# A dynamic convolution and a tanh-shrink layer on one core: ScalarE products in the ramp, more helping tokens, two tap sums from superblock 9, and stores ahead of loads

## The chip, the core and the metric

The kernel runs on one core of a Trainium2 chip. The metric is device time in microseconds (us). Seven names are used: TensorE (PE in the profile; its weight loads are PEld), VectorE (DVE), ScalarE (ACT), GpSimd (POOL), SyncE (SP, which here only issues transfers), SBUF (the memory that all engines read) and PSUM (the banks into which TensorE writes).

## The reference

Two stages over 32768 tokens (8 sequences of 4096) of 192 values.

```python
w = softmax(weight_gen, axis=-1)            # 8 heads x 7 taps for each token
x_pad = 6 zero rows ahead of each sequence
conv[s, head] = sum over k of w[s, head, k] * x_pad[s + k, head]   # 24 values a head
h = conv @ w_in                              # 192 x 2048
out = (h - tanh(h)) @ w_out                  # 2048 x 192
```

Inputs and output are float32.

## The kernel before, in words

The tokens are cut into 32 superblocks of 1024 (`TOK`): 128 partitions with 8 tokens (`J`) each. A sequence is four superblocks. The function is one long program, an order written out by hand: each engine takes its instructions in the order in which the code issues them, and waits only where data or a buffer is not ready.

**Making the convolution.** A superblock n needs `x` (8 rows and a halo of 6 in each partition, `load_x`, L144), its seven weights for each token and head (`load_wg`, exp on ScalarE L185, sum L199, reciprocal L208 or L214 and scaling L250 on VectorE or GpSimd), and seven products, one for each tap: x shifted by k times weight k (`tap_product`, L264). GpSimd makes nearly all of them. Taps 0 to 3 go to a tile `pa`, taps 4 to 6 to `pb`, both bf16. `pa` has three buffers, `pb` one. Superblocks 0 and 1 share their products between VectorE (V) and GpSimd (G_) by written lists (L687 and L722).

**Adding the taps.** GpSimd issues transfers that add while they write (`dma_sum`, L256): the first sum adds `pb` to `pa[0:3]`, so that four products are left. For superblocks in `TWO_SUMS` a second sum adds `pa[2:4]` to `pa[0:2]`, so that two are left. The second sum of n is issued after the first products of n + 1 (`second_sum`, L358). TensorE adds what is left while it transposes: `conv_sums` (L419, matmul L436) multiplies every product by the identity into the same PSUM columns, 24 matmuls for each product, and ScalarE evicts to `convT` (L462, in the ramp L454). Superblock 0 and 1 have seven products in this step, 2 and 3 five, 4 to 10 four, 11 and later two.

**The two matmuls.** For each superblock `gemm1` (L474) makes 16 tiles f of 128 of the 2048 columns: six matmuls into a PSUM tile `ph` (three buffers, L496), tanh on ScalarE into `th` (L509), and the difference on VectorE into `gt` (L510). The second matmul, `out_stream` (L550, L564), takes a block of 128 tokens over all 16 `gt`; its two halves of 64 rows run side by side, one block apart, and ScalarE evicts each block (L583). In the loop over n (L803) every step f issues `gemm1(n, f)`, then a number of steps of the second matmul of superblock n - 1 (the `pairs` of a plan), and in between, at the f that the plan names, the transposes of superblock n + 1 (`t2` for its first two chunks of 64 values, `t1` for the third) and the softmax of n + 3 or n + 4.

**Who sets the place of what.** `products(n + 2)` is issued at f = 1 of n; its part `rest` (L359: the products 4 to 6, the first sum, and for superblocks in `LAST_TAP` tap 3 behind that sum) follows later in the step. For superblocks in `LOCKED` the first sum waits for the VectorE instruction of f = 10 (L374). `HELP` (L56, L292) takes tokens from GpSimd: at step f = 3 of n - 2 VectorE makes the product of the last token for taps 0 and 1. `load_x(n + 3)` waits for the first product of n + 2 (`x_after`); its place against the store of superblock n - 1 depends on `STORE_FIRST` (L849, L873): up to n = 8 the store is issued first, later the load. SyncE issues loads and stores in that order.

**Ramp.** Superblock 0's transposes come before any other matmul; ScalarE copies the first 7 of 16 column tiles of `w_in` from the lower to the upper 64 partitions (L712), the rest comes by a transfer (L719). The transposes of superblock 1 lie between the tiles of superblock 0 (`EARLY` and `THIRD`, L742).

**End.** After the last tile the second matmul of the last superblock runs in `gemm2_last` (L598): for each block both halves write one PSUM tile, ScalarE copies the one, VectorE adds the other, and every second block is stored.

Of the kernel before, what the change touches and what calls it, by code (L numbers as in the profile page):

```python
# [8 lines left out]
FP32 = mybir.dt.float32  # L9
# [7 lines left out]
def kernel(  # L17
# [27 lines left out]
    PART = (2, 3)  # L45
    TWO_SUMS = tuple(range(11, 32))
    THREE = ()
    AHEAD = 4
    STORE_FIRST = 8
    EXTRA = (5, 9, 11, 13)  # L50

    WG_AT = 9
    LOCK, LOCKED = 10, tuple(range(14, 32))
    WARM = 0
    SUM_LATE, SUM_BEHIND = (), ()
    HELP = {n: ((n - 2, 3, 2),) for n in range(4, 32)} | {n: ((n - 2, 3, 2), (n - 3, 12, 2)) for n in (9, 10)}  # L56
    CUTS0 = [0, 2, 4]
    LAST_TAP = (4, 5, 6, 7, 8)
    X_LATE = ()
# [3 lines left out]
    RELIEF = ()  # L63
    ACT_OPS = {}
    ACT_AT = {}
    BOTH = False
    RAMP_TAPS = (((True, 6, 7), (False, 2, 6), (True, 0, 2)), ((True, 4, 7), (False, 0, 2), (True, 2, 4)))
    W_CUTS = ((0, 3),)
# [136 lines left out]
    def softmax_recip(n, j0=0, j1=J):  # L205
        if j0 == 0:
            zr_of[n] = wgpool.tile([P, J * H], FP32, name="zr")
        nc.vector.reciprocal(zr_of[n][:, j0 * H : j1 * H], zsum_of[n][:, j0 * H : j1 * H])  # L208

    def softmax_norm(n, bank):  # L210

        wsm = softmax_tile()
        zr_v = bank[:, 512 - J * H : 512]
        nc.vector.reciprocal(zr_v, zsum_of[n][:])  # L214

        def finish():
            scale(nc.vector, wsm[:], e_of[n], zr_v)

        wsm_of[n] = (wsm, None, None, None)
        return finish  # L220
# [60 lines left out]

    def act_product(n, j, k, h):

        x_t, wsm, pa = hold(n)
        nc.scalar.activation(
            out=pa[:, k, j, h * G : (h + 1) * G],
            in_=x_t[:, k + j, h * G : (h + 1) * G],
            func=ACT.Copy,
            scale=wsm[:, j, h, k : k + 1],
        )  # L290

    def help(n, ph, j, kh):  # L292

        x_t, wsm, pa = hold(n)
        w = ph[:, 0, 0 : kh * H].rearrange("p (k h) -> p k h", k=kh)
        nc.vector.tensor_copy(w, wsm[:, j].rearrange("p h k -> p k h")[:, 0:kh])
        tap_product(nc.vector, pa[:, 0:kh], x_t, w, (H, 1), 0, kh, j, j + 1)

    def products(n, taps=None, sums=None, hooks={}):
# [8 lines left out]
        if n == 1:  # L308

            last = [opool.tile([P, 2, J, D], BF16, name="pb1", tag="out_sb") for _ in range(2)]  # L310
            home = [(pa, 0, KA), (last[0], KA, KA + 2), (last[1], KA + 2, K)]
        else:
            pb = pbpool.tile([P, K - KA, J, D], BF16, name="pb")
            home = [(pa, 0, KA), (pb, KA, K)]
# [24 lines left out]

        end = KA - 1 if n in LAST_TAP else KA  # L340
        left = [J - sum(kh > k for _, _, kh in HELP.get(n, ())) for k in range(KA)]
        for j, k in {(j, k) for j, k, _ in ACT_OPS.get(n, ())}:
            left[k] = min(left[k], j)

# [13 lines left out]
        second_sum(n - 1)  # L358
        def rest():  # L359
            if n in PART:  # L360
                dma_sum(pa[:, 0:2], pa[:, 2:4])
            if n - 1 in whole:
                mul(nc.gpsimd, KA, K - 1)
                third_sum(n - 1)
                mul(nc.gpsimd, K - 1, K)
            else:
                mul(nc.gpsimd, KA, K)
            if n in PART:
                prods_of[n] = parts(4, 5, 6, 0, 1)
            else:  # L370
# [4 lines left out]

                if n in LAST_TAP and n in SUM_BEHIND:
                    most(KA - 1, KA)
                    first_sum()
                elif n in SUM_LATE:
                    sum_of[n] = first_sum  # L380
                else:
                    first_sum()
                    if n in LAST_TAP:
                        most(KA - 1, KA)
                if n in TWO_SUMS:
# [8 lines left out]
        return rest  # L394

    def second_sum(n):

        if n in to_sum:
            pa = to_sum.pop(n)
            dma_sum(pa[:, 0:2], pa[:, 2:4])  # L400
            if n in THREE:
                whole[n] = pa

    def third_sum(n):

        if n in whole:
            pa = whole[n]
            dma_sum(pa[:, 0:1], pa[:, 1:2])

    def turn(n):  # L410
# [136 lines left out]
    half = {}  # L547
    out_of = {}

    def out_stream():  # L550
# [46 lines left out]

    def gemm2_last(j, f0=0, f1=NFT):  # L598

        n = NTOT - 1  # L600
        if f0 == 0:
            half[j] = psum_h.tile([P, 2, HT], FP32, name="po2", tag="ph")
        po = half[j]
        col = (j % 2) * HT + (j // 2) * P
        for f in range(f0, f1):
            for r in range(2):
                nc.tensor.matmul(  # L607
# [5 lines left out]
                )  # L613
        if f1 < NFT:
            return
        if j == 0:
            out_of[n] = opool.tile([P, J, D], FP32, name="out_sb")
        out_sb = out_of[n]
        if BOTH:
            nc.vector.tensor_add(out_sb[:, j, :], po[:, 0, 0:D], po[:, 1, 0:D])  # L620
        else:
            ot = tpool.tile([P, D], FP32, name="ot", tag="th")
            nc.scalar.activation(out=ot[:], in_=po[:, 0, 0:D], func=ACT.Copy)
            nc.vector.tensor_add(out_sb[:, j, :], po[:, 1, 0:D], ot[:])
        if j in STORES:
            j0 = max([s for s in (-1, *STORES) if s < j]) + 1
            nc.sync.dma_start(
                out=tokens(out, n)[:, j0 : j + 1, :],
                in_=out_sb[:, j0 : j + 1, :],
            )  # L630

# [49 lines left out]
    for c0, c1 in W_CUTS:  # L681
        load_w_in(c0, c1, 0, FA, last_exp[0] if c0 == 0 else None)
    softmax_norm_ramp(0, obank[0])
    products(
        0,
# [9 lines left out]
            (V, 2, 3, 0, J),  # L695
            (G_, 1, 2, 0, J),
        ],
        sums=(6, 5, 4, 3, 0, 2, 1),
        hooks={1: rest_of_w_in},
    )  # L700

    SOFT_EARLY = False
    if SOFT_EARLY:
        load_wg(2)
    load_x(1, first_halo[0])
    if not SOFT_EARLY:
        load_wg(2)
    softmax_exp(1)
    load_wg(3)

    for c in range(NC):
        nc.scalar.activation(out=w_in[R:P, c, 0:FA], in_=w_in[0:R, c, 0:FA], func=ACT.Copy)  # L712
    if SOFT_EARLY:
        softmax_exp(2)
    softmax_norm_ramp(1, obank[1])
    if SOFT_EARLY:
# [4 lines left out]
        1,  # L721
        taps=[(V, 0, 1, 0, J), (V, 1, 2, 0, J), (G_, 4, 6, 0, J), (G_, 6, 7, 0, J), (G_, 2, 4, 0, J)],  # L722
        sums=(0, 1, 4, 5, 6, 2, 3),
        hooks={6: load_w_out},
    )
# [4 lines left out]
    if not SOFT_EARLY:  # L730
        softmax_norm_ramp(2, obank[0])
    products(2)()

# [3 lines left out]

    load_wg(4)
    load_x(3)
    PER = 4 * JH  # L740

    EARLY, THIRD = ((7, 3), (9, 1), (11, 7)), 13  # L742
    for f in range(NFT):
        if f in RELIEF:
            relieved = gemm1_relieved(0, f)
        else:
            gemm1(0, f)
        for lag, step in ((1, 0), (2, 1)):
# [27 lines left out]
    LATE, LATE_FROM = STEADY, 99  # L776
    DOUBLE_IN = tuple(range(4, 10))
    TURNED = dict(pairs=(5, 11, 0, 16, 3, 13, 6, 10, 0, 6, 10, 5, 11, 5, 11, 16), t1=(16, 0), t2=(16, 0), scale=14, sums=(1, 7))
# [21 lines left out]
    wg_next = [6]  # L800

    rest = None
    for n in range(1, NTOT):  # L803
        more = n < NTOT - 1
        finish = []
        turned = n + 1 in THREE
        plan = TURNED if turned else FIRST if n == 1 else DOUBLE if n in DOUBLE_IN else APART if n in APART_IN else LATE if n >= LATE_FROM else STEADY

        soft = [m for m in (n + 3 if n <= AHEAD else n + 4,) if m < NTOT]
        for f in range(NFT):  # L810
            ph = gemm1(n, f)
            if n == 1:
# [5 lines left out]
                for at, (step, m, h) in zip(plan["sums"], [s + (h,) for s in steps for h in (0, 1)]):  # L818
                    if f == at:
                        step(m, h * JH, (h + 1) * JH)  # L820
                if f == 5:
                    wsm_of[3] = (softmax_tile(), None, e_of[3], zr_of[3])
# [8 lines left out]
            if n > 1:  # L831
                for h, at in enumerate(plan["sums"]):
                    if soft and f == at:
                        softmax_sum(soft[0], h * JH, (h + 1) * JH)
            if n == AHEAD:
                for at, (step, h) in zip(EXTRA, [(s, h) for s in (softmax_sum, softmax_recip) for h in (0, 1)]):
                    if f == at:
                        step(n + 4, h * JH, (h + 1) * JH)
                if f == EXTRA[-1]:
                    wsm_of[n + 4] = (softmax_tile(), None, e_of[n + 4], zr_of[n + 4])  # L840
            for m in (n + 2, n + 3):
                for j, k, h in [o for o, at in zip(ACT_OPS.get(m, ()), ACT_AT.get(m, ())) if at == (n, f)]:
                    act_product(m, j, k, h)
                for t, (a, b, kh) in enumerate(HELP.get(m, ())):
                    if (a, b) == (n, f):
                        help(m, ph, J - 1 - t, kh)
            if n + 2 < NTOT and f == (9 if n == 1 else LOCK if n + 2 in LOCKED else max([b for a, b, _ in HELP.get(n + 2, ()) if a == n] + [3])):
                rest()
# [28 lines left out]

    gemm2_last(0, 0, J)
    out_pairs(NFT)
    gemm2_last(0, J, NFT)  # L880
    for j in range(1, J):
        gemm2_last(j)

# [29 lines left out]
```

## Time and profile before

| what | value |
|---|---|
| median of 3 runs | 740.5 us (739.93 to 740.76) |
| profiled execution | 740.35 us, its span 738.5 us |
| TensorE busy | 719.4 us, 97% of the span |
| VectorE busy | 685.0 us, 93% |
| GpSimd busy | 658.8 us, 89%, nothing after 685 us |
| ScalarE busy | 638.3 us, 86% |
| granted TensorE clock | 1.00 |
| transfers | 131.02 MB, 177 GB/s mean |

The span is what the profiler recorded; the execution's own time is 1.85 us longer. Busy time sums the instructions of an engine, and an engine with a high share need not set the end: the part of the page on the chain that ended last follows the work back from the last instruction and says whom it waited for. Idle time is listed with what ended it. A row of a timeline gives start, length, engine, line, operation, output and input with their shapes, the count, and in brackets the idle time before it and its releaser.

### The profile page before, as it was taken

The page shows a single profiled execution, that of the slowest core. Times are in us where ns is not written, and L with a number is a line of the kernel's source. Part 1 is how long each engine was busy: PE and PEld are TensorE (multiplying, and loading weights), DVE is VectorE, ACT ScalarE, POOL GpSimd, SP SyncE. Part 2 cuts the span into 40 slices and gives each one's busy share as a digit, 9 for nine tenths or more (in the row PEclk, how much of TensorE's full clock was granted, in tenths as well). Part 3 has the DMA queues.
Part 4 walks back from the last instruction along what each step waited for, and adds up shares of the span by engine and source line. Part 5 has one row for each costly group of instructions (what it writes and reads, how often), then busy time and mean ns, then how long its engine had stood idle before and what let it go on. Part 6 is the DMA issues. An engine that isn't in the chain of part 4 may idle for free.

```text
span 738.5 us, 29833 instructions
## 1 busy us (share of the span) xinstructions
PE 719.4 (97%) x13520; PEld 553.2 (75%) x13520; DVE 685.0 (93%) x718; ACT 638.3 (86%) x871; POOL 658.8 (89%) x163
## 2 busy tenths in 40 slices
PE   3899999999999999999999999999999999999997
PEld 2477877777777777777777777777777777777777
DVE  7999999999999999999999999999999999988893
ACT  4888888888888899989898999898998989888983
POOL 7999999999999999999999999999999999995000
PEclk9999999999999999999999999999999999999999
DMA  7925367666466997778898888898878889766312
GB/s 205 248 46 162 134 169 192 184 169 154 132 183 176 226 231 196 170 183 205 212 236 197 181 183 201 205 231 219 187 174 193 207 217 225 192 144 110 88 44 87
DMA packets 34780, 131.02 MB, mean 177 GB/s; under 512 B 4591, under 2 KB 9439, under 8 KB 30814
## 3 DMA queue, kind: packets, MB, share of 16 engines
q0 software_dynamic: 19936, 52.69, 40.7%
q1 hardware_dynamic: 14718, 76.44, 30.4%
q8 instruction: 105, 1.72, 0.9%
q14 instruction: 21, 0.17, 0.1%
HBM read 53.93 MB, written 25.17 MB: 107 GB/s over the span
## 4 chain that ended last, share of the span: by engine, by line
PE 94%; DVE 4%; ACT 1%; issue 1%; DMA 0%
PE obank L564 45%; PE ph L496 44%; PE pc L436 4%; PE po L607 1%; DVE gt L510 1%; DVE pa L268 1%; ACT th L509 0%; DVE pb L268 0%; DMA wg_t<-in_weight_gen_dram 0%; DVE obank L227 0%; DVE zsum L199 0%; DVE wsm L250 0%; ACT wg_t L185 0%; ACT convT L454 0%; DVE obank L250 0%
## 5 line engine op out<-in xcount | busy, mean ns | idle before, releaser
L510 DVE TENSOR_TENSOR gt<-ph,th 128x1024 bf16<-128x1024 f32 x512 | 601.2, 1218 | 32.5 <-ACT th L509 22.9
L509 ACT ACTIVATE th<-ph 128x1024 f32<-128x1024 f32 x512 | 513.1, 1026 | 66.0 <-PE ph L496 54.9
L496 PE MATMUL ph<-convT,w_in 64*128 64x512 bf16 x3072 | 415.1, 379 | 3.7 <-DVE gt L510 2.4
L564 PEld LDWEIGHTS <-gt 64*128 64x128 bf16 x7936 | 354.6, 94 | 81.9 <-issue 7.1
L564 PE MATMUL obank<-w_out,gt 64*128 64x192 bf16 x7936 | 406.8, 243 | 0.9 <-issue 0.8
L268 POOL TENSOR_TENSOR pa<-x_ring,wsm 128x2688 bf16<-128x2688 f32 (+3 forms) x66 | 330.4, 5258 | 0.2
L268 POOL TENSOR_TENSOR pb<-x_ring,wsm 128x4608 bf16<-128x4608 f32 (+2 forms) x32 | 275.5, 8612 | 1.5 <-DVE obank L250 1.0
L496 PEld LDWEIGHTS <-w_in 64*128 64x128 bf16 x3072 | 160.8, 94 | 83.9 <-issue 16.8
L583 ACT ACTIVATE out_sb<-obank 128x192 f32<-128x192 f32 x248 | 81.2, 327 | 10.5 <-PE obank L564 10.0
L462 ACT ACTIVATE convT<-pc 128x1024 bf16<-128x1024 f32 (+1 forms) x62 | 50.2, 811 | 4.4 <-PE pc L436 4.3
L257 POOL DMA_DIRECT2D pa<-pb x28 | 35.9, 1284 | 11.9 <-POOL pb L268 9.2
L257 POOL DMA_DIRECT2D pa<-pa x23 | 38.1, 1656 | 8.9 <-DMA pa<-pb 8.2
L436 PEld LDWEIGHTS <-pa 64*128 64x128 bf16 x1968 | 40.3, 101 | 6.1 <-POOL pa L268 0.9
L436 PE MATMUL pc<-ident,pa 64*128 64x64 bf16 x1872 | 39.8, 192 | 1.3 <-POOL pa L268 0.8
L199 DVE TENSOR_REDUCE zsum<-wg_t 128x32 f32<-128x224 f32 (+1 forms) x61 | 23.6, 387 | 2.9 <-ACT wg_t L185 2.9
L185 ACT ACTIVATE wg_t<-wg_t 128x448 f32<-128x448 f32 x32 | 18.2, 569 | 6.4 <-DMA wg_t<-in_weight_gen_dram 6.4
L250 DVE TENSOR_TENSOR wsm<-wg_t,pc 128x448 f32<-128x448 f32 x27 | 16.8, 621 | 2.5
L268 DVE TENSOR_TENSOR pa<-x_ring,ph 128x384 bf16<-128x384 f32 x30 | 16.6, 554 | 1.3
L214 DVE RECIPROCAL pc<-zsum 128x64 f32<-128x64 f32 x27 | 14.8, 550 | 0.0
L436 PE MATMUL pc<-ident,pb 64*128 64x64 bf16 x216 | 4.9, 206 | 9.0 <-POOL pb L268 9.0
L436 PEld LDWEIGHTS <-pb 64*128 64x128 bf16 x288 | 6.3, 107 | 9.5 <-POOL pb L268 9.0
L607 PE MATMUL po<-w_out,gt 64*128 64x192 bf16 x256 | 11.2, 243 | 0.0
(28 smaller groups left out, 74.5 us busy)
## 6 DMA issues: line engine op xcount, KB each, us to landing
x_ring<-in_x_dram SPq DMA_DIRECT2D x29, 1344.0 KB, 8.4
pa<-pb POOLq DMA_DIRECT2D x28, 1152.0 KB, 9.9
out_dram<-out_sb SPq DMA_DIRECT2D x31, 768.0 KB, 7.7
pa<-pa POOLq DMA_DIRECT2D x23, 768.0 KB, 9.8
wg_t<-in_weight_gen_dram SPq DMA_DIRECT2D x32, 224.0 KB, 8.1
x_ring<-in_x_dram SPq DMA_DIRECT2D x2, 768.0 KB
x<-in_x_dram SPq DMA_DIRECT2D x1, 1344.0 KB, 7.3
w_out<-in_moe_w_out_dram POOLq DMA_DIRECT2D x1, 768.0 KB, 9.6
```

The costliest lines, as they stand in the source:

```text
L185: last_exp[0] = nc.scalar.activation(out=wg_t[:].rearrange("p j h k -> p (j h k)"), in_=wg_t[:].rearrange("p j h k -> p (j h k)"), func=AC ...
L199: nc.vector.reduce_sum(out=zsum_of[n][:, j0 * H : j1 * H], in_=e_of[n][:, j0:j1].rearrange("p j h k -> p (j h) k"), axis=AX.X,)
L257: return nc.gpsimd.dma_start(out=out.rearrange("p k j d -> p k (j d)"), in_=in_.rearrange("p k j d -> p k (j d)"), accum_op=mybir.AluOpTyp ...
L268: return eng.tensor_mul(bass.AP(tensor=out.tensor, offset=out.offset + j0 * D, ap=[out.ap[0], [J * D, nk], [G, run], [1, G]]), bass.AP(ten ...
L436: nc.tensor.matmul(pc[r][:, col : col + R] if home else pc[:, r, col : col + R], lhsT=prods[c][gi][r * R : (r + 1) * R, 2 * j : 2 * j + 2] ...
L462: last_conv[0] = nc.scalar.activation(out=out, in_=pc[:, :, 0:cols].rearrange("p r (cj t) -> p r cj t", t=R), func=ACT.Copy,)
L496: nc.tensor.matmul(ph[:, r, :], lhsT=w_in[r * R : (r + 1) * R, c, ff], rhs=convT[r * R : (r + 1) * R, c, :], start=(c == 0), stop=(c == NC ...
L509: last_act[0] = nc.scalar.activation(out=th[:], in_=ph_f, func=ACT.Tanh)
L510: last_sub[0] = nc.vector.tensor_sub(gt[:], ph_f, th[:])
L564: mm = nc.tensor.matmul(po[:, 0:D], lhsT=g_of[n][f][r * R : (r + 1) * R, col : col + P], rhs=w_out[r * R : (r + 1) * R, f, :], start=(r == ...
L583: last_act[0] = nc.scalar.activation(out=out_sb[:, j, :], in_=po[:, 0:D], func=ACT.Copy)
L607: nc.tensor.matmul(po[:, r, 0:D], lhsT=g_of[n][f][r * R : (r + 1) * R, col : col + P], rhs=w_out[r * R : (r + 1) * R, f, :], start=(f == 0 ...
```

## The change

It has these parts.

- **Ramp.** In superblock 0 GpSimd makes tap 1 for four of eight tokens; ScalarE makes the other four (`ACT0`): two tokens ahead of its copies of `w_in`, two behind. In superblock 1 VectorE makes tap 1 for four tokens, and ScalarE the other four (`ACT1`) behind the tanh of tile f = 2. A token is 8 Copy activations of 128x24, one for each head, with the weight as scale (`act_product`). The load of x and of the weights for superblocks 3 and 4 is issued behind f = 2. The third chunk of superblock 1 is transposed at f = 14 instead of 13.
- **Helping tokens.** Superblocks 5 to 9 have two tokens helped by VectorE (at f = 3 and f = 12 of the superblock two before), 4 and 10 one, 11 to 13 none, 14 and later one as before. ScalarE makes one more token of tap 3 for superblocks 5 and 7 and of tap 2 for 6, at f = 12.
- **Two tap sums** from superblock 9 instead of 11. The plans of 8 and 9 become those of later superblocks (transposes at f = 13 instead of 11).
- **Order.** Superblock 8 has its tap 3 with the other products; the first sum of 14 no longer waits for f = 10; all stores are issued ahead of the x load of the same step; softmax sums of single superblocks move by a step or two.
- **End.** Each 64-row half of a block of the last superblock has its own PSUM tile, and the lower half runs six matmuls ahead of the upper one.

Many new names have empty values and do nothing: `SINGLE`, `FILL`, `PART_FILL`, `SCALE_EARLY`, `REST2`, `PB2`, `X1_EARLY`, `SOFT1_AT`, `WOUT_CAST`, and `EXTRA_NORM` is off. `SUM_BEHIND` names superblock 11, which is not in `LAST_TAP`, and does nothing either. The diff, cut to its core:

```diff
-    TWO_SUMS = tuple(range(11, 32))
+    TWO_SUMS = tuple(range(9, 32))
-    STORE_FIRST = 8
-    EXTRA = (5, 9, 11, 13)
+    STORE_FIRST = 31
+    EXTRA = ((4, 5), (4, 9), (4, 11), (4, 15))
-    LOCK, LOCKED = 10, tuple(range(14, 32))
+    LOCK, LOCKED = 10, tuple(range(15, 32))
-    HELP = {n: ((n - 2, 3, 2),) for n in range(4, 32)} | {n: ((n - 2, 3, 2), (n - 3, 12, 2)) for n in (9, 10)}
+    HELP = {2: (), 4: ((2, 3, 2, 1),), 5: ((3, 3, 2, 1), (3, 12, 2, 1)), 6: ((4, 3, 2, 1), (4, 12, 2, 1)), 7: ((5, 3, 2, 1), (5, 12, 2, 1)), 8: ((6, 3, 2, 1), (6, 12, 2, 1)), 9: ((7, 3, 2, 1), (7, 12, 2, 1)), 10: ((8, 3, 2, 1),), 11: (), 12: (), 13: (), 14: ((12, 3, 2),), 15: ((13, 3, 2),),
...
-    LAST_TAP = (4, 5, 6, 7, 8)
+    LAST_TAP = (4, 5, 6, 7)
+    ACT_HELP = {5: ((3, 12, 3),), 6: ((4, 12, 2),), 7: ((5, 12, 3),)}
+    ACT0 = ((7, 0), (6, 0), (5, 3), (4, 3))
+    ACT1 = ((7, 2), (6, 2), (5, 2), (4, 2))
+    ACT1_TAP = 1
+    X3_AT = 2
+    SKEW = 6
+    TAPS1 = ((True, 0, 1, 0, 8), (True, 1, 2, 0, 4), (False, 4, 6, 0, 8), (False, 6, 7, 0, 8), (False, 2, 4, 0, 8))
+    EARLY, THIRD = ((7, 3), (9, 1), (11, 7)), 14
...
+    def act_product(n, j, k):
         x_t, wsm, pa = hold(n)
-        nc.scalar.activation(
-            out=pa[:, k, j, h * G : (h + 1) * G],
+        for h in range(H):
+            nc.scalar.activation(
+                out=pa[:, k, j, h * G : (h + 1) * G],
+                in_=x_t[:, k + j, h * G : (h + 1) * G],
+                func=ACT.Copy,
+                scale=wsm[:, j, h, k : k + 1],
+            )
...
-            (G_, 1, 2, 0, J),
+            (G_, 1, 2, 0, J - len(ACT0)),
...
-    for c in range(NC):
-        nc.scalar.activation(out=w_in[R:P, c, 0:FA], in_=w_in[0:R, c, 0:FA], func=ACT.Copy)
+    for c in range(NC + 1):
+        for j, at in ACT0:
+            if c == at:
+                act_product(0, j, 1)
+        if c < NC:
+            nc.scalar.activation(out=w_in[R:P, c, 0:FA], in_=w_in[0:R, c, 0:FA], func=ACT.Copy)
...
-            gemm1(0, f)
+            helpers(0, f, gemm1(0, f))
+        for j, at in ACT1:
+            if f == at:
+                act_product(1, j, ACT1_TAP)
+        if f == X3_AT:
+            load_wg(4)
+            load_x(3)
...
-    gemm2_last(0, 0, J)
-    out_pairs(NFT)
-    gemm2_last(0, J, NFT)
-    for j in range(1, J):
-        gemm2_last(j)
+    rows = [last_rows(r) for r in range(2)]
+    for _ in range(J):
+        for r in rows:
+            next(r)
+    for f in range(NFT):
+        out_pairs(1)
+        if f >= NFT - SKEW:
+            next(rows[0])
+    for _ in range(J * NFT - J):
+        for r in rows:
+            next(r, None)
+    for _ in rows[1]:
+        pass
```

`last_rows(r)` is the old `gemm2_last` as a generator for one half r: it allocates its own `po2` tile for each block, ScalarE copies half 0 when that half ends, and VectorE adds half 1 when that one ends. The plans (`PLANS`) give superblocks 1 to 13 their own lists; those of 8 to 13 have the transposes at f = 13, and 5 and 7 differ from before by one step of the second matmul.

## The prediction

> **What bounds the kernel now.** I read the shares of the chain that ended last, then that chain over the first 60 us, then the timelines of ScalarE, GpSimd and TensorE. The page's chain by engine:
>
> ```profile
> PE 94%; DVE 4%; ACT 1%; issue 1%; DMA 0%
> ```
>
> TensorE carries the end. The table of busy time by 10 us shows it at 10.00 of 10 from 40 us on (except 9.23 at 240 to 250) and at 0.97, 7.76, 8.31 and 8.50 before. What delays work before 40 us is therefore paid in full, and after it every TensorE instruction counts. In the ramp the chain (start, us, engine and output) runs through VectorE:
>
> ```profile
> 20.38 1.14 DVE gt L510
> 21.52 0.04 issue
> 21.56 2.76 PE ph L496 x12
> 24.32 0.02 issue
> 24.34 1.03 ACT th L509
> 25.38 0.02 issue
> 25.40 8.04 DVE gt L510 x7
> ```
>
> One loop holds it: `ph` has three buffers, so tile f+3 waits for the `gt` of f, then for ScalarE's `th`, then for VectorE. VectorE takes 1.16 us a tile (9 in 10.44 us), ScalarE 0.92 to 0.97 (two in 1.94). ScalarE's lead is small; its rows with the idle before them:
>
> ```profile
> 9.01 0.58 ACT L185 ACTIVATE wg_t<-wg_t 128x448 f32<-128x448 f32 x1 [5.05 <-DMA wg_t<-in_weight_gen_dram]
> ...
> 10.53 2.63 ACT L712 ACTIVATE w_in<-w_in 64x896 bf16<-64x896 bf16 x3 [0.94 <-DMA w_in<-in_moe_w_in_dram]
> ...
> 15.40 1.51 ACT L462 ACTIVATE convT<-pc 128x1024 bf16<-128x1024 f32 x2 [2.24 <-PE pc L436]
> ...
> 20.64 1.02 ACT L509 ACTIVATE th<-ph 128x1024 f32<-128x1024 f32 x1
> ...
> 23.07 1.02 ACT L509 ACTIVATE th<-ph 128x1024 f32<-128x1024 f32 x1 [1.40 <-PE ph L496]
> ...
> 24.12 10.44 DVE L510 TENSOR_TENSOR gt<-ph,th 128x1024 bf16<-128x1024 f32 x9 [0.35 <-ACT th L509]
> ...
> 41.22 0.17 ACT L508 ACTIVATE once<-ph 128x1 f32<-128x1 f32 x1 [0.60 <-PE ph L496]
> 41.28 1.94 ACT L509 ACTIVATE th<-ph 128x1024 f32<-128x1024 f32 x2
> ```
>
> The gaps of 0.94, 2.24 and 1.40 us are exactly where the change puts 16, 16 and 32 new activations.
>
> **Part 1, the ramp on ScalarE.** New: 64 Copy activations of 128x24 with a scale from SBUF. No row shows this form, so I bound its interval a. Per element ScalarE takes (1026 - 327) / (1024 - 192) = 0.84 ns, so 24 elements are 0.02 us. Below: `th` starts 0.06 us after `once`, so a = 0.08. Nearest in kind are the three back-to-back copies from SBUF to SBUF at 10.53: (2.63 - 0.92) / 2 = 0.86 us apart, less 896 x 0.84 = 0.75, leaves 0.11, so a = 0.13. Above, with no overlap, an isolated 128x192 copy is 0.327 - 168 x 0.00084 = 0.19. I take 0.13 and keep 0.08 and 0.19.
>
> Superblock 0: 16 run from 9.59 to 11.7, ahead of the `w_in` copies, which end at 14.3 instead of 13.16; the other 16 end at 16.4. GpSimd does its half of tap 1 by 13.3, but TensorE's last tap needs both halves: it began at 14.75, now 16.4, and the first `ph` moves by 1.65 us. Superblock 1: VectorE saves half a tap of 1.7 us, is free at 19.5 instead of 20.38, and gains nothing since `th` of tile 0 now comes at 20.65. `th` of tile 2 ends at 23.5 (21.66 before, with the exp of superblock 3 at its heels), then 32 x 0.13 = 4.1 us, then `th` of tile 3 until 28.6. Its `gt` starts at 28.65 instead of 24.12: **+4.5 us**. The loop gains only 0.2 us a tile and its lead is at most 0.3, and the two evictions at 33.00 drain that anyway, so nothing is recovered before 40 us. At a = 0.08 the first batch is hidden, `th` of tile 2 ends at 21.9, and 2.5 us follow: `gt` at 25.45, +1.3. At 0.19: first tile +3.6, `gt` of tile 3 at 32.6, +8.5.
>
> The Trainium skill, ScalarE: Activation LUTs, section What ACT_TABLE_LOAD costs, states 186 ns + 0.833 ns per element for an ACTIVATE, about 93 ns more per pointer operand, and about 93 ns of overlap between neighbours. The 1026 ns of `th` agree with its first term (1039). By it a is 0.206 and my sum becomes 749.7 us.
>
> **Part 2, second tap sums from superblock 9.** Superblocks 9 and 10 lose two of four products each: 96 transposing matmuls. Their price is read from one superblock to the next with four and with two products:
>
> ```profile
> 184.67 1.38 PE ph L496 x12
> ...
> 207.17 1.38 PE ph L496 x12
> ...
> 274.96 1.38 PE ph L496 x12
> ...
> 296.81 1.38 PE ph L496 x12
> ```
>
> 22.50 against 21.85, so **-1.3 us** for two. The price is two more sums on GpSimd (21.68 us a superblock with it, 20.43 without: 1.25 each), and their landing (9.1 to 10.3 us).
>
> **Part 3, helping tokens, and whether GpSimd is in time.** GpSimd multiplies at 1.82 ns per element (10.49 us for 5760). Helpers take 576 elements each from superblocks 5, 6, 7 and 384 from 8: -3.9 us. The 0.7 us it gains in superblock 0 are capped: its `pb` of superblock 4 already waited 0.18 us for TensorE at 81.72, so from there it moves with TensorE. Superblocks 10 to 13 each lose one helped token, +0.7 each. The rows that matter (GpSimd's product and second sum, TensorE's first transposes):
>
> ```profile
> 207.47 8.62 POOL L268 TENSOR_TENSOR pb<-x_ring,wsm 128x4608 bf16<-128x4608 f32 x1
> ```
> ```profile
> 248.11 1.72 POOL L257 DMA_DIRECT2D pa<-pa  x1
> ...
> 259.57 0.65 PE L436 MATMUL pc<-ident,pa 64*128 64x64 bf16 x32
> ```
>
> In all that follows the ramp's shift moves both sides. The sum of 9 can start at 207.47 - 3.9 + 0.7 = 204.3 and lands by 214.5; TensorE asks at 211.2 + 2.4 (two tiles and 13 block pairs later in the new plan) + 0.4 (below) = 214.0. For 12 the start is 269.80 - 3.9 + 2.5 + 2.8 = 271.2, landing 281.3, asked for at 281.42 - 1.3 + 0.4 = 280.5. So the second sums come 0 to 1.0 us late, once, not each time; I take **+0.5**. If the wait of 0.8 us for the sum's landing ahead of `pb` of 7 (143.76) goes and the sums land in 9.1, it is nothing; at 14 the removed order gives back the 1.01 us that GpSimd waited at 302.58.
>
> On VectorE superblocks 3, 4 and 5 get one more helper, 0.75 us (113.06 to 113.81). In 4 it is not covered: 16 x 1.163 + four half sums at 0.30 + two half reciprocals at 0.28 + softmax 1.29 + two helpers 1.5 = 23.2 against TensorE's 22.5, and it ran 22.76 before: **+0.4** (0 to 0.7). Three batches of 8 activations cost ScalarE 1.0 us each; a tile's `gt` ends about 1.1 us before TensorE needs the buffer, which hides them (without that cover 0.1 to 0.5 each).
>
> **Part 4, the end.** TensorE keeps 144 steps of 0.084 us. ScalarE's last copy leaves the end: -0.36 (0.33 + 0.03). But each row half now has its own bank buffer, and r1 of block j+1 waits for the copy of r0 of j: 0.24 + 0.05 + 0.33 + 0.05 = 0.67 us after r0's last matmul starts, and seven steps are 0.59. Seven waits of 0.08 are +0.6; together **+0.2** (-0.4 to +0.6, as matmul ends are modelled).
>
> **Part 5, stores ahead of x loads.** From superblock 9 SP now holds the load behind the store: 264.79 becomes 268, landing 8.4 us later at 276.7, and GpSimd reads it at 281.0. Covered by 4.3 us; price 0. Were it not, the transfer would meet the second sum (269.80) and cost up to 1.5. The moved sums, reciprocals and third chunk issue the same instructions: 0, behind VectorE's 0.3 us of idle per superblock.
>
> **Sum.** +4.5 - 1.3 + 0.5 + 0.4 + 0.2 = +4.3 on the profiled execution's 740.35 us (span 738.5 and 1.85 around it): 744.65. That execution lies 0.15 below the median of 740.5. I forecast **744.6 us**.
>
> **Rivals.**
> - *Cheap activations* (a = 0.08): +1.3 in place of +4.5, 741.4 us. For it: 0.06 us at 41.22. Against: that is one element from PSUM with no pointer.
> - *The gaps hold them* (a at or under 0.06): superblock 0's batches fit 0.94 and 2.24 us, tap 1 is done by 14.2, `gt` of tile 3 stands at 24.1, and GpSimd gets its full help: -1.3 - 0.4 on the tail, 738.6 us. For it: the gaps are there. Against: no row shows two activations from SBUF closer than 0.86 us. It decides from a = 0.06 down; from 0.08 up part 1 alone eats part 2's saving.
> - *Isolated price* (a = 0.19): +8.5, so 748.7 us. For it: each of the 64 reads its own scale from memory, which no row does. Against: every back-to-back row overlaps. The rule of the Trainium skill quoted in part 1 would make this rival true.
> - *Late sums*: landing of 12.2 us, the longest row, makes +2 in part 3: 743 if the ramp costs only 1.3.
>
> **Chances.** Forecast 0.38, cheap 0.17, gaps 0.27, isolated with the late sums 0.18. About 0.2% (1.5 us) is what a measurement can tell here. Slower: 0.38 + 0.18 + 0.06 of the cheap case = 0.62; within: 0.10 + 0.02 = 0.12; faster 0.26. The range takes the gaps' case from 738.4 up to the isolated one at 749.0; the forecast's own is 742.5 to 746.5.
>
> **What would show it.** ScalarE's row of 16 at 9.6 and of 32 after the third `th`: their length is a. Right: `gt` of tile 3 near 28.6, TensorE idle before it over 4 us, superblocks 8 and 9 at 21.85. Wrong: 32 of them in under 2 us, or TensorE's transposes of 9 to 13 waiting for a transfer by over 1 us each.

## The result, and the profile after

The kernel after takes 764.5 us (median of 6 runs, 762.89 to 769.38) beside 740.47 for the kernel before in the same runs: ratio 1.0335, 95% interval 1.0305 to 1.0364. It is 24.0 us slower, far above the forecast of 744.6 and its range. The profiled execution took 766.13 us, with a span of 764.4.

The chain of work that ended last is the first line to set beside the one of before. Shares of the span:

```profile
PE 51%; POOL 22%; DMA 13%; ACT 5%; DVE 4%; issue 3%; SPq 0%; POOLq 0%; ACTq 0%; DVEq 0%
```

TensorE carried 94% before. Now a third of the end is set by GpSimd's products and by transfers, so something new holds TensorE in the steady stage, where the prediction had priced the new store order at nothing. ScalarE's share went from 1% to 5%. The same chain in the ramp (start, us, engine and output), kernel after:

```profile
26.18 4.13 ACT pa L327 x21
...
32.73 0.92 ACT th L587
...
33.67 1.24 DVE gt L588
...
34.95 2.75 PE ph L574 x12
```

VectorE's `gt` carried this stretch before; now ScalarE's new activations do, and the `gt` of tile 3 starts at 33.67 instead of 24.12. ScalarE's timeline of the kernel after (start, us, line, operation, output and input, count):

```profile
9.91 3.38 ACT L327 ACTIVATE pa<-x_ring,wsm 128x24 bf16<-128x24 f32 x16
13.29 2.63 ACT L800 ACTIVATE w_in<-w_in 64x896 bf16<-64x896 bf16 x3
...
26.07 6.66 ACT L327 ACTIVATE pa<-x_ring,wsm 128x24 bf16<-128x24 f32 x32
```

A second batch of 16 follows at 15.93. One activation lasts 0.303 us, so the interval from one to the next is (6.66 - 0.303) / 31 = 0.205 us: 32 of them take 6.66 us and not 4.1.

To see where the rest came from, the store of each superblock is a good marker: SP issues one in each, in the order of the work. Its start in the kernel after less its start in the kernel before:

| store (start before, us) | shift in the kernel after, us |
|---|---|
| 66.26 / 87.25 | +9.1 / +12.1 |
| 155.17 | +15.5 |
| 223.12 / 267.98 | +16.5 / +15.4 |
| 333.54 | +16.3 |
| 464.66 | +21.8 |
| 639.03 | +25.3 |

So there are three main losses: the ramp (the first tanh of superblock 1 comes 10.3 late), superblocks 3 to 5 (1.1 to 1.2 each), and from 333 to 639 us another 9.0 that come in steps, most of them small. The remaining 2.6 lie between these. The last stage shows in the waits (in all, times, longest us) and the transfers (count, KB each, median us from issue to landing), first of the kernel after, then the second sum's row of the kernel before:

```profile
PE pc L514 <- DMA pa<-pa: 8.7, 13, 1.8
```
```profile
x_ring<-in_x_dram SPq DMA_DIRECT2D x29, 1344.0 KB, 10.0
...
out_dram<-out_sb SPq DMA_DIRECT2D x31, 768.0 KB, 4.0
pa<-pa POOLq DMA_DIRECT2D x25, 768.0 KB, 11.6
```
```profile
pa<-pa POOLq DMA_DIRECT2D x23, 768.0 KB, 9.8
```

The second sum (`pa<-pa`) took 9.8 us to land before, the x load 8.4, the store 7.7: the first two are 1.8 and 1.6 slower, the store 3.7 quicker. Every second sum's landing is in the trace; of the x loads and the stores of the steady stage it tells only two or three each. TensorE waited 13 times for a second sum, 8.7 us in all; before there was no such wait.

### The profile page after: what moved, and what is told of

It is laid out like the page before. It is cut to its first block, busy times and chain, and to the rows that moved or that the text cites. A ratio compares the mean times of both kernels' runs of the same rounds, so it can differ in the third digit from the quotient of the medians.

```text
span 764.4 us, 29751 instructions
## 1 busy us (share of the span) xinstructions
PE 720.9 (94%) x13424; PEld 552.0 (72%) x13424; DVE 684.7 (90%) x718; ACT 657.4 (86%) x959; POOL 658.9 (86%) x164
## 4 chain that ended last, share of the span: by engine, by line
PE 51%; POOL 22%; DMA 13%; ACT 5%; DVE 4%; issue 3%; SPq 0%; POOLq 0%; ACTq 0%; DVEq 0%
PE obank L643 24%; PE ph L574 23%; POOL pa L297 16%; DMA pa<-pa 13%; DVE gt L588 4%; POOL pb L297 4%; PE pc L514 3%; ACT pa L327 2%; POOL pa L286 2%; ACT th L587 2%; PE po L687 1%; DMA wg_t<-in_weight_gen_dram 1%; ACT w_in L800 0%; SPq L172 0%; ACT convT L532 0%
## 5 line engine op out<-in xcount | busy, mean ns | idle before, releaser
L297 POOL TENSOR_TENSOR pa<-x_ring,wsm 128x3072 bf16<-128x3072 f32 (+3 forms) x65 | 327.9, 5293 | 0.2
L514 PEld LDWEIGHTS <-pa 64*128 64x128 bf16 x1872 | 37.3, 101 | 25.6 <-issue 16.9
L286 POOL DMA_DIRECT2D pa<-pa x25 | 41.6, 1663 | 10.0 <-DMA pa<-pb 9.4
L327 ACT ACTIVATE pa<-x_ring,wsm 128x24 bf16<-128x24 f32 x88 | 18.6, 303 | 0.0
```

Source lines behind the costliest of these rows:

```text
L286: return nc.gpsimd.dma_start(out=out.rearrange("p k j d -> p k (j d)"), in_=in_.rearrange("p k j d -> p k (j d)"), accum_op=mybir.AluOpTyp ...
L297: return eng.tensor_mul(bass.AP(tensor=out.tensor, offset=out.offset + j0 * D, ap=[out.ap[0], [J * D, nk], [G, run], [1, G]]), bass.AP(ten ...
L327: nc.scalar.activation(out=pa[:, k, j, h * G : (h + 1) * G], in_=x_t[:, k + j, h * G : (h + 1) * G], func=ACT.Copy, scale=wsm[:, j, h, k : ...
L514: nc.tensor.matmul(pc[r][:, col : col + R] if home else pc[:, r, col : col + R], lhsT=prods[c][gi][r * R : (r + 1) * R, 2 * j : 2 * j + 2] ...
```

## The experiments

Theory A: the ramp's activations cost 10 us, the helper bursts on ScalarE 3, and the new order on SP's queue the rest, since it brings the x load onto the second sum. The rivals are in the expectations. The kernel before was run again beside every group of kernels (medians 740.63 to 741.57), and a ratio is to it.

**One part undone at a time.**

```diff
- ACT0 = ((7, 0), (6, 0), (5, 3), (4, 3))
- ACT1 = ((7, 2), (6, 2), (5, 2), (4, 2))
- TAPS1 = (..., (True, 1, 2, 0, 4), ...)
+ ACT0 = ()
+ ACT1 = ()
+ TAPS1 = (..., (True, 1, 2, 0, 8), ...)
```

The last line gives VectorE tap 1 of superblock 1 for all eight tokens again.

> The changed kernel with no ScalarE products in superblocks 0 and 1: GpSimd and VectorE make all of tap 1 again. In the changed trace the first tanh probe of superblock 1 comes at 51.4 us against 41.2 before. Theory A (the 64 short activations cost the ramp 10 us, and all of it is paid at the end): the probe is back near 41 us and the time falls by 9 to 10.5 us, to about 754.5. Rival B (GpSimd and its sums are late anyway from superblock 9 on, so that a later TensorE was partly hidden): the probe is back as well, but the time falls by 5 us or less, to 759 or more, and TensorE's waits for the second sums grow.

757.02 us, ratio 1.0191 (1.0151 to 1.0231): 7.5 back by the medians, 8.7 between the profiled executions and 10.7 by the ratios. B's 5 or less is out, and A's 9 to 10.5 is neither met nor ruled out: the four runs go from 751.1 to 757.39. The markers are 12.3 earlier up to 333 us (+4.0 instead of +16.3), and then this kernel loses 12.8 where the kernel after lost 9.0.

```diff
- STORE_FIRST = 31
+ STORE_FIRST = 8
```


> The changed kernel with the old order on SyncE from superblock 9 on: the x load ahead of the store of the same step. Theory A (the load behind the store now moves beside GpSimd's second sum, which lands in 11.6 us instead of 9.8, and TensorE waits for it in most superblocks): the median landing of the second sums is back under 10.5 us, TensorE's waits for them nearly vanish, and the time falls by 8 to 10 us, to about 755.5. Rival B (GpSimd is late from 9 on because of two more sums and four superblocks without helped tokens, whatever the order of the loads): the waits stay and the time is within 2 us of 764.5.

757.56 us, ratio 1.0220 (1.0198 to 1.0241): 6.9 back by the medians, 8.5 by the ratios. The second sums land in 9.6 us again, and the shift stays put: +16.4 at 333.54, +17.2 at 639.03. So of the 9.0 us that the steady stage lost from 333 to 639, all but 0.7 go with this one line. That is A's mechanism, at a size near the lower end of its 8 to 10.

```diff
- ACT_HELP = {5: ((3, 12, 3),), 6: ((4, 12, 2),), 7: ((5, 12, 3),)}
+ ACT_HELP = {}
```


> The changed kernel without the three helped tokens of ScalarE for superblocks 5, 6 and 7 (GpSimd makes them). Theory A: TensorE's three idle stretches of 0.7, 0.9 and 0.9 us in superblocks 3, 4 and 5, each behind 8 short activations of 1.6 us, go, and the time falls by 2.5 us, to 762. Rival B (GpSimd needs the 0.35 us a token more than ScalarE costs): same or slower, 764 to 766.

765.99 us, ratio 1.0318 (1.0283 to 1.0353), not told apart from the kernel after: by the time, B. The markers of the profiled execution are 2.6 us earlier at 155.17 (+12.9 instead of +15.5), as A said, but that execution was the quickest of the four by far (761.29, the others 765.46 to 766.92), so the total shows neither theory. What the bursts do stands in the kernel after, in ScalarE's and then TensorE's timeline:

```profile
112.67 1.74 ACT L327 ACTIVATE pa<-x_ring,wsm 128x24 bf16<-128x24 f32 x8
114.32 0.31 ACT L662 ACTIVATE out_sb<-obank 128x192 f32<-128x192 f32 x1
```
```profile
114.67 0.84 PE L643 MATMUL obank<-w_out,gt 64*128 64x192 bf16 x16 [0.72 <-ACT out_sb L662]
```

Eight activations stand ahead of the copy that empties a bank of the second matmul, and TensorE waits for that bank, three times (0.72, 0.92 and 0.93). Without the bursts no such wait is in the trace.

```diff
- scale=wsm[:, j, h, k : k + 1],
+ scale=0.25,
```


> The changed kernel with a constant 0.25 as the scale of ScalarE's products in place of the weight from memory: those products are wrong, their number, shape and place are the same. The changed trace has the 32 of them 0.205 us apart, 0.303 us each. Theory P (0.09 us of that is the scale's pointer, as the Trainium skill, ScalarE: Activation LUTs, section What ACT_TABLE_LOAD costs, says): each takes 0.21 us, 32 of them last 3.6 us instead of 6.7, and with both batches of superblock 0 shorter by 1.5 us each the time falls by 5 to 7 us, to about 758.5. Rival Q (a short activation costs 0.2 us whatever its scale): 6.6 us for 32 as now, and 764.5.

This kernel leaves the weights out of these products. 755.55 us (2 runs), ratio 1.0190 (1.0166 to 1.0214), which is 9.0 less by the medians, more than the 5 to 7 of P. Its ScalarE timeline:

```profile
9.81 1.90 ACT L327 ACTIVATE pa<-x_ring 128x24 bf16<-128x24 f32 x16
...
22.86 3.70 ACT L327 ACTIVATE pa<-x_ring 128x24 bf16<-128x24 f32 x32
```

One lasts 0.213 us, so the interval is (3.70 - 0.213) / 31 = 0.112 us instead of 0.205. So P's mechanism is shown, and Q is out: the scale read from memory costs 0.09 us in each activation, which is the term that the prediction's nearest row lacked.

**The parts put together, and one at a time on a clean base.** Ramp, bursts and queue order undone at once:

> The kernel after with three parts undone at once: ScalarE makes no tap in the ramp (VectorE has its whole tap 1 of superblock 1 back), no helper batch in superblocks 3 to 5, and every x load is issued ahead of the store of the superblock before it. What stays of the change: the new order of superblocks 1 to 13, VectorE's helping tokens, second sums from 9, the new end. Theory A (the ramp about 9 to 10 us, the bursts about 3, the order of SP's queue 7 to 9; all else about -1): 739 to 741 us, ratio 0.998 to 1.001, second sums landing in about 9.7 us again, the probe of superblock 1 at 40.9. Rival B (the new plans of the early superblocks leave GpSimd late, whatever the three parts do): 745 us or more, with TensorE waiting for second sums over 5 us in all.

743.78 us, ratio 1.0037 (1.0024 to 1.0049). Neither: 2.8 above A's upper bound, and four waits for second sums, 4.3 us in all (1.79, 0.69, 0.84, 0.98). The first and the last of them in TensorE's timeline:

```profile
216.76 0.65 PE L514 MATMUL pc<-ident,pa 64*128 64x64 bf16 x32 [1.79 <-DMA pa<-pa]
...
306.79 0.65 PE L514 MATMUL pc<-ident,pa 64*128 64x64 bf16 x32 [0.98 <-DMA pa<-pa]
```

The same with `TWO_SUMS` from 11:

> As the kernel with three parts undone, and second tap sums from superblock 11 as before. Theory A (part 2 of the prediction: 0.65 us for each of two superblocks): 1.3 us above the kernel with three parts undone; superblocks 8 and 9 from one x12 burst to the next 22.5 us instead of 21.85. Rival B (the saved transposes are given back, since GpSimd and the second sums of 9 and 10 come late): within 0.5 us of it.

740.94 us, ratio 1.0002 (0.9993 to 1.0011). Both theories missed: the second sums of 9 and 10 do not save 1.3 us here, they cost 2.8. This kernel is level with the kernel before, so what is left in it (VectorE's helping tokens, the plans, the new end) costs nothing together, and it is the clean base. Put back on it, the whole ramp:

> The kernel with three parts undone and second sums from 11 (740.9 us), with ScalarE's 64 activations of the ramp put back and nothing else. Theory A (0.205 us each: 32 after the third tile's th take 6.7 us, TensorE starts 10 us late and never gets it back): 750 to 752 us, ratio 1.012 to 1.015, probe of superblock 1 near 51. Theory of the prediction (0.13 each, +4.5): 745.4. Rival B (GpSimd, relieved of half a tap of superblock 0, and a loop with a lead give part of it back before superblock 8): 746 to 749.

751.51 us, ratio 1.0146 (1.0132 to 1.016): +10.6 alone, as A said. With the old queue order the shift stays at +11.0 from 267.98 to 639.03. Of the ramp, the first 32 alone (`ACT1 = ()`):

> The same base with ScalarE's 32 activations of superblock 0 alone; VectorE keeps its whole tap 1 of superblock 1. Theory A (two batches of 3.4 us: the w_in copies end 2.8 us later, the tap of superblock 0 and its transposes follow, and the first th moves by that): 743.5 to 745 us, ratio 1.004 to 1.006, so the 32 of superblock 1 are the dearer half by far. Rival B (the wait of 2.24 us ahead of the convT copies absorbs the first batch): within 1 us of the base.

743.22 us, ratio 1.0030 (1.0018 to 1.0042): +2.3, just below A's bounds and outside B's, so the 32 of superblock 1 add 8.3. And ScalarE's bursts, put back on the version with three parts undone:

> The kernel with three parts undone (743.8 us; second sums from 9), with ScalarE's three helper batches of 8 put back. Theory A (each holds the output bank's copy back and costs TensorE 0.7 to 0.9 us, three times 1.1 us by the markers; the relief of GpSimd is not worth it since the second sum of 9 was 1.8 us late): +1 to +2.5 us, 745 to 746.3. Rival B (the 1.05 us that GpSimd saves brings the second sums of 9 to 13 in time and pays for the batches): 743 us or less.

745.81 us, ratio 1.0069 (1.0056 to 1.0083): +2.0, A.

**The queue order.** In the kernel before, `STORE_FIRST = 31` and nothing else:

> The kernel before with one edit: from superblock 9 on the store is issued ahead of the x load, as in the kernel after. Theory A (the order by itself brings the x load onto the second sum): 747 to 753 us, ratio 1.009 to 1.017, second sums landing in over 11 us instead of 9.8, the loss growing from superblock 12 to the end. Rival B (the order is harmless while TensorE is on time, since store and load then still start 1 to 5 us ahead of the second sum; only a late TensorE brings them together): within 1.5 us of the kernel before. My prediction's part 5 (covered by 4.3 us) is B.

752.3 us, ratio 1.0147 (1.0124 to 1.017): +11.4 by one line, A. Its transfers, and the second sums that lie on its chain (start, us):

```profile
pa<-pa POOLq DMA_DIRECT2D x23, 768.0 KB, 12.0
```
```profile
269.50 14.31 DMA pa<-pa
360.00 13.31 DMA pa<-pa
405.78 11.90 DMA pa<-pa
```

The x load started at 270.36, 359.68 and 404.45 (SP's queue): 0.9 us after the sum, 0.3 ahead of it, 1.3 ahead; the later the load, the longer the sum. In the kernel before it starts 5.0 us ahead (374.43 and 379.44), and the sums land in 9.8. The kernel after shows the same within one trace: where the load starts 3.3 to 5.0 us ahead of a second sum (superblocks 9 to 15), the sum lands in 7.5 to 10.6 us; where it starts 0.7 to 2.2 ahead, in 11.5 to 13.0; the one time it starts 1.1 behind, in 14.4. To bring the two together without touching the order on the queue, in the kernel before:

```diff
- x_after[n + 1] = first
+ x_after[n + 1] = m if n > 8 else first
```

Here `m` is the second product and `first` the first.

> The kernel before with one edit: from superblock 9 on each x load is released by the second of GpSimd's two products of its first tile instead of the first, so it starts about 5 us later, with the second sum, and on SP's queue it is still ahead of the store. Nothing else moves. Theory A (what costs time in the new order is that the x load runs at the same time as the second sum, which then takes 11.6 to 14 us instead of 9.7): second sums landing in over 11 us, TensorE waiting for them in many superblocks, 745 to 753 us. Rival B (it is the queue: what the load is held behind, not when it runs): within 1.5 us of the kernel before, since the load still has some 10 us until GpSimd reads it.

789.54 us, ratio 1.0667 (1.0651 to 1.0683): +48.9, far above A's 745 to 753, with A's mechanism; B is out. Its transfers, a sum on its chain, and the x load on SP's queue that belongs to it:

```profile
x_ring<-in_x_dram SPq DMA_DIRECT2D x29, 1344.0 KB, 7.6
...
pa<-pa POOLq DMA_DIRECT2D x23, 768.0 KB, 14.6
```
```profile
367.44 15.03 DMA pa<-pa
```
```profile
368.00 0.33 SPq L155 DMA_DIRECT2D x_ring<-in_x_dram  x1
```

The load is ahead of the store here and is issued 0.56 us after the sum; the nine sums on its chain take 14.1 to 15.2 us, and the two loads of the steady stage whose landing the trace tells took 7.6 us each (8.4 and 9.3 in the kernel before). TensorE's waits for second sums (in all, times, longest us):

```profile
PE pc L436 <- DMA pa<-pa: 29.1, 11, 3.9
```

The long ones come in every second superblock. So it is when the load runs, not what it stands behind. But not all of the 46.4 us by which this span is longer are these waits. TensorE's busy time is 732.4 us instead of 719.4: beside each of the seven waits of 2.8 to 3.9 us the granted clock was 0.5 for 3.4 or 6.8 us (from 330.92 for 6.83 us the first time), and 1.00 elsewhere in the steady stage. And 4.0 us were lost in superblock 3, ahead of the first load that the edit moves. So the size of this run is no price of the meeting alone.

**The second sums from 9.** In the kernel before alone:

> The kernel before with one edit: second tap sums from superblock 9 instead of 11, and nothing done to relieve GpSimd. Theory A: GpSimd pays 1.25 us each for two more sums and second sums come late until its order is removed: 740 to 742 us, with waits of TensorE for second sums at 9 to 14. Rival B: GpSimd's order has room, and it keeps the 1.3 us: 739.2 us.

748.37 us, ratio 1.0100 (1.0087 to 1.0114): worse than both theories. It is one event. TensorE's timeline:

```profile
217.68 1.04 PE L436 MATMUL pc<-ident,pa 64*128 64x64 bf16 x32 [6.75 <-DMA pa<-pa]
```

The shift is -0.5 at 200.19, +7.4 at 223.12, and about +7 from there to the end. Its plan asks for the transposes of 9 early: TensorE was ready at 210.93, and GpSimd had issued the sum only at 207.78. With the new plans, second sums from 10:

> The kernel with three parts undone, second tap sums from 10 instead of 9: superblock 9 keeps four products on TensorE (+0.65 us), GpSimd has one sum less (1.25 us) before its order is removed. Theory A (what was lost is GpSimd's lateness at 9 and 11 to 13, 4.3 us of waits; without the sum of 9 the largest wait of 1.8 us goes and the later ones shrink): 740.5 to 742, between the versions from 9 (743.8) and from 11 (740.9). Rival B (the sum of 10 alone fits GpSimd's slack): 740.3, faster than the kernel before.

742.42 us, ratio 1.0023 (1.0013 to 1.0032): between the two as A said, 0.4 above its bound. The sum of 10 alone costs as well: 1.5 above the base. Why GpSimd is late stands in its timeline in the version with three parts undone, and in VectorE's:

```profile
195.65 1.29 POOL L286 DMA_DIRECT2D pa<-pb  x1 [2.11 <-issue]
...
206.94 1.72 POOL L286 DMA_DIRECT2D pa<-pa  x1
...
229.31 1.72 POOL L286 DMA_DIRECT2D pa<-pa  x1
```
```profile
194.55 0.55 DVE L297 TENSOR_TENSOR pa<-x_ring,ph 128x384 bf16<-128x384 f32 x1
```

GpSimd waits 2.11 us ahead of the first sum of 9, and starts it 0.55 us after VectorE's helping token ended. The profile names no releaser; the helping token writes into the same `pa`. The token of 9 that was made at tile 12 of superblock 6 is now made at tile 12 of superblock 7. And GpSimd's own round, 229.31 - 206.94 = 22.37 us, is longer than TensorE's 21.85, so it falls back by another 0.5 in each superblock. Moving the token back alone:

```diff
- 9: ((7, 3, 2, 1), (7, 12, 2, 1))
+ 9: ((7, 3, 2, 1), (6, 12, 2, 1))
```


> The kernel with three parts undone (743.8 us; second sums from 9) with one edit: VectorE's second helping token of superblock 9 is made at tile 12 of superblock 6, as in the kernel before, and not at tile 12 of superblock 7. In its profile GpSimd stood 2.11 us at 195.65 ahead of the first sum of 9, 0.55 us after that helping token ended (194.55 + 0.55), and the second sums of 9, 11, 12 and 13 came 1.79, 0.69, 0.84 and 0.98 us late. Theory A (the helping token that came late holds the first sum, and GpSimd never makes that up, since its 22.36 us a superblock exceed TensorE's 21.85): the 2.11 go, the second sum of 9 is issued near 204.9, the four waits of 4.3 us go or fall under 1 us in all, and the time is 739.3 to 740.5 us, below the kernel before. Rival B (it is GpSimd's rate and the extra sums, not the helping token): 743 us or more, with waits for second sums over 3 us.

742.10 us, ratio 1.0018 (1.0009 to 1.0027): between A and B. The 2.11 go, but the second sum of 9 starts only 0.86 us earlier (206.08), and three of the four waits stay, smaller: 0.27, 0.48 and 0.83. So 1.7 of the 2.8 us are the token; that the rest is GpSimd's longer round fits the waits, but no run isolates it. With one more early token for 10, `10: ((8, 3, 2, 1), (7, 12, 2, 1))`:

> The same, and a second helping token for superblock 10 at tile 12 of superblock 7. Theory A (each helping token saves GpSimd 0.7 us and costs VectorE 0.75 where TensorE doesn't wait for it): within 0.5 us of the one before it, since its waits are gone already, or below it by what waits were left at 11 to 13. Rival (VectorE's extra token in superblock 7 holds TensorE's tile back): 0.5 to 1 us above.

741.42 us, ratio 1.0003 (0.9994 to 1.0012), level with the kernel before and within A. One wait of 0.38 is left, and now the saving is there. TensorE's pairs of tiles, one superblock apart, in this kernel:

```profile
209.61 1.52 PE L574 MATMUL ph<-convT,w_in 64*128 64x512 bf16 x12
...
231.91 1.48 PE L574 MATMUL ph<-convT,w_in 64*128 64x512 bf16 x12
...
253.73 1.47 PE L574 MATMUL ph<-convT,w_in 64*128 64x512 bf16 x12
```

22.30 and 21.82 us, against 22.47 and 22.40 (207.93, 230.40, 252.80) in the base with second sums from 11: 0.75 less, 1.13 without the wait. It is spent before 209 us, where two helping tokens in one tile cost TensorE 0.64 at 173.30 (the hold that the rival named) and a stall that the profile names nothing for 0.72 at 204.04. The token two tiles later:

> The kernel with the two early helping tokens (741.4 us) with the token of superblock 9 made at tile 14 of superblock 6 instead of tile 12, where VectorE made two in a row and TensorE waited 0.64 us at 173.30. Theory A: that wait goes, the second sum of 9 stays within 0.4 us of its time, 740.8 us, level with the kernel before. Rival: the token two tiles later holds GpSimd's first sum, 741.5 to 743.

741.11 us, ratio 1.0012 (1.0003 to 1.0021): not told apart from the one before it. A is not borne out: the wait at the helping tokens does not go but is 0.47, and a wait of 0.71 for a second sum comes back at 303.91. No version tried is faster than the kernel before.

## Why the prediction was wrong, step by step

| step | predicted, us | measured, us | from |
|---|---|---|---|
| ramp | +4.5 | +10.6 | whole ramp on the clean base |
| second sums from 9, with GpSimd's lateness | -1.3 + 0.5 | +2.8 | second sums from 9 against from 11 |
| ScalarE's batches | 0 | +2.0 | batches put back |
| helping tokens on VectorE, plans | +0.4 | +0.1 with the end | clean base against before |
| end | +0.2 | -0.05 | traces |
| stores ahead of x loads | 0 | +6.9 to +8.5 | undone in the kernel after |
| sum | +4.3 | +22.4 to +24.0 | kernel after: +24.0 |

The measured parts add up to about the whole, but they were taken on different bases (the store order alone costs 11.4 in the kernel before), so this is no check to the microsecond. The direction came out for the forecast's main reason, the ramp, at less than half its size; the other 13 us come from steps that the prediction priced at nothing or as a gain.

- **Part 1 failed by a term of its sum.** The chain of events is as forecast (the copies of `w_in` late, then `th` of tile 3 held by 32 activations, nothing recovered), but a, the interval, is 0.205, not 0.13. All 64 activations stand in that chain, so 64 x 0.075 = 4.8 us are missing from the term, and 4.5 + 4.8 = 9.3: the `gt` of tile 3 came 33.67 - 24.12 = 9.55 later. The rest up to 10.6 is not separated; TensorE's granted clock was 0.5 for 6.83 us from 31.04 in the kernel after, beside its wait of 6.63 us for this `gt`; in the kernel before and with the first 32 alone it was 1.00 from 25 us on. The row it was read from, copies that read no scale from memory, lacks 0.09 us: with a constant the interval is 0.112. That row was right for what it showed, and it was the wrong row. By the figures of the Trainium skill (ScalarE: Activation LUTs, section What ACT_TABLE_LOAD costs) the interval is, as an estimate, 0.206, and 0.113 without the pointer to a scale. The traces agree with both, 0.205 and 0.112. The rival of 0.19 was the nearest of the four. The argument against it, "every back-to-back row overlaps", was true and left out what the memory scale adds: 0.303 - 0.205 = 0.10 us of overlap against 0.09 us for the scale.
- **Part 2 holds as a saving** (1.13 of 1.3 us once GpSimd is in time), but not as a result. The words "late, once, not each time" failed. The working had GpSimd's round at 21.68 plus 0.7 for the token that is lost, 22.38, and TensorE's at 21.85, and added this up as far as superblock 12, but priced it as one wait. The version with three parts undone has four, 4.3 us in all.
- **Part 3 failed twice.** The relief of 3.9 us from 5 to 8 was counted whole, without asking when the helping token of 9 comes: GpSimd stood idle for 2.11 us until just after it, and the second sum of 9 started at 206.94, not 204.3. And ScalarE's batches were hidden by the wrong cover: the slack of `gt` and the `ph` buffers, where the copy of the output bank was the nearer thing behind them.
- **Part 4**: from the first matmul of the stream of last rows to the last addition it is 12.77 us after (748.66 to 761.43) and 12.82 before (722.74 to 735.56). The waits of 0.08 at each block were not there at that size: ScalarE's copies are 1.34 us apart instead of 1.32.
- **Part 5 failed in the step that gave it the price 0.** The cover of 4.3 us was that of the reader, GpSimd's next product, and it held. The sentence after it named the right danger, that the load would meet the second sum, as what happens if the cover fails; but the meeting does not depend on the cover. Before, the load left 5.0 us ahead of the sum; behind the store it leaves 0.7 to 2.2 ahead from superblock 16 on, and once 1.1 behind. "Up to 1.5" was the size of one meeting (the waits of TensorE from there on are 0.23 to 0.94 us); it comes in most superblocks, and the order cost +6.9 to +8.5.

Three things stay open. The loss of the steady stage with the new order, from 333 to 639 us, is 9.0 in the kernel after, 12.8 without the ramp, 6.6 without the bursts, 8.3 in the kernel before with that order: the later TensorE is, the later its store lets the load go, so lead and lateness can feed each other, but no run fixes what sets the size. It may be why the ramp and the bursts, undone in the kernel after, did not give back 10.6 and 2.0. Of the 9.0, the waits for second sums are 5.7 us; TensorE also stood for 1.77 us at 483.54 with no releaser in the profile, and similar stalls stand in the traces without the ramp (1.76) and without the bursts (1.49). And no run says which resource the load and the sum share.

## What to carry to other kernels

Price a new small instruction by a row with the same operands, not only the same size: where it reads a scale from memory and the row doesn't, not even the price without any overlap (0.19 here) is an upper bound: 0.205 was measured. When a transfer is moved, ask not only whether its reader still gets it in time but which other transfer it will now run beside, and how often. For a relief of an engine, look at when the helper's own instruction is done, and compare the rounds of the two engines: half a microsecond longer per round is a wait in every round, and not one.

## What the hardware showed that was not expected

A load of 1344 KB issued some 0.6 us after a sum of 768 KB stretches the sum from 9.8 us to between 14.1 and 15.2, while two such loads land in 7.6 us (8.4 and 9.3 before): by these few, the sum pays and the load does not. That is not so for every order: with the store right ahead of it, one load issued 1.6 us after a sum took 12.4 us (store first, in the kernel before). Issued 5.0 us ahead it leaves the sum's median at 9.5 to 9.9. And an activation of 24 elements costs the same 0.205 us of ScalarE's time wherever it stands, in the ramp or in the steady stage (1.74 us for 8 are 0.303 and seven times 0.205), of which 0.09 is the scale that it reads. And a long wait of TensorE cost more than itself: beside waits of 2.8 to 6.75 us in the steady stage the granted clock was 0.5 for 3.4 or 6.8 us (run with the later load, and second sums from 9 in the kernel before), and beside waits of at most 2.3 us there it stayed at 1.00.
